# One group of sink scores for two units, sink rows of v by GpSimd transfers, and a new order of work

## The chip, the cores and the metric

The kernel runs on one core of a Trainium2 chip. The metric is device time in microseconds, as a median over several runs. All times of the profile come from one profiled execution and are counted from the start of its span.

## What is computed

Windowed attention with a few always-visible "sink" keys, followed by a channel-mix feed-forward block, for 4 sequences of 768 positions, 8 heads of 64:

```python
scores = scale * q @ k.T                       # per sequence and head
keep   = (key position < 4) | (0 <= query - key < 128)
a      = softmax(where(keep, scores, -1e9))
x      = (a @ v), heads side by side           # [4, 768, 512]
x_prev = x shifted by one position
xk, xr = mu_k*x + (1-mu_k)*x_prev, mu_r*x + (1-mu_r)*x_prev
k      = relu(xk @ w_k)                        # 512 -> 1024
out    = sigmoid(xr @ w_r) * ((k*k) @ w_v)     # 1024 -> 512, and 512 -> 512
```

Inputs and output are float32; the products run in bfloat16.

## The kernel before

A *unit* is 256 positions of one sequence, so there are 12 units, and unit `u` is the part `T = u % 3` of sequence `b = u // 3`. For each unit the kernel does five stages, each made of small operations:

- **load**: k, q and v rows by transfers that SyncE (SP) issues (line 337 for k and q, line 307 for v); the feed-forward weights come by line 354 in five transfers of 1 MB and are cast to bfloat16 by `cast` (line 501 on ScalarE, 505 and 507 on VectorE).
- **prepare**: cast k, q and v to bfloat16 (lines 536 to 543 and 646), turn k and q so that the head dimension lies on the partitions, in early units by TensorE (`transpose`, line 576, four 128x128 pieces) with a copy out of PSUM (`evacuate`, line 589), in later ones by a transposing transfer.
- **attend**: for two head pairs at a time the scores (line 721), the exponential on ScalarE (line 775), the mask on VectorE (line 789; units 0 and 1 add a bias by TensorE instead, line 728), the products with v (line 808), the reciprocal and the division (lines 822 and 825).
- **mix**: turn x by TensorE (line 849), copy it out (line 858), difference and two interpolations on VectorE (lines 877 and 888).
- **ffn** of the unit before: keys (line 939), relu (949 or 953), square (963 or 967), gate (979) with tanh (985), product (997, for the last half unit 909), last multiplication (1006, 919) and the store.

**Sinks.** The window of a unit with T > 0 doesn't reach the first four keys, so they are handled apart. `sink_keys` (line 670, GpSimd) copies the four key columns of every head into `ksink`, zero elsewhere. `sink_scores` (line 696) multiplies them by q of one unit: four matmuls of 256 columns, one for each head pair, each filling 32 of the 128 partitions of a bank. One exponential (line 703) gives `es`. The line 676 matmul `spread` x `vb` puts the four sink rows of v where `es` needs them, and line 680 multiplies by `hmask` into `vsink` on VectorE. `sink_values` (line 763) then adds es x vsink to the outputs. Groups of sink scores exist for T = 1 and for T = 2: eight in all. There is one `ksink`/`vsink` pair for each sequence.

**Order.** Every operation has a number, in the order in which the program text creates it. `CHOICE` says which engine takes an operation that several could do, `ORDER` is the order in which all are issued (each engine keeps its part of that order), `SLOTS` says which buffer of a pool each takes. All three were written by a planner. A negative number in `ORDER` is a filler: a 512-column matmul on zeros (line 1018) that does no work of the reference. `ORDER` holds 30 of them. SP's and GpSimd's queues are in order too: what waits at the head holds up what is behind it.

**GpSimd at the start** makes the constants: `make_ident`, `make_hmask`, `make_bias0`, `make_bias1`, `make_spread`, `make_mask`, `make_mask0`, `make_sinks`. VectorE first does the fills `fill` (with `ones`) and `fill_later` (with `ksink` and `vsink`).

Of the kernel before, what the change touches and what calls it, by code (L numbers as in the profile page):

```python
# [18 lines left out]
    92: "ACT", 93: "ACT", 94: "ACT", 95: "ACT", 97: "ACT", 100: "ACT", 102: "DVE", 105: "DVE",  # L19
    110: "DVE", 111: "DVE", 114: "ACT", 115: "DVE", 139: "POOL", 142: "POOL", 145: "POOL", 148:  # L20
    "DVE", 150: "DVE", 151: "ACT", 152: "ACT", 154: "DVE", 161: "DVE", 191: "DVE", 193: "DVE",
    194: "DVE", 197: "DVE", 199: "DVE", 200: "DVE", 203: "DVE", 204: "DVE", 213: "DVE", 230:
    "ACT", 234: "ACT", 273: "DVE", 276: "DVE", 279: "DVE", 282: "DVE", 285: "ACT", 286: "ACT",
    298: "DVE", 306: "DVE", 315: "ACT", 354: "DVE", 364: "ACT", 365: "DVE", 367: "DVE", 383:
    "ACT", 387: "ACT", 436: "DVE", 439: "DVE", 444: "DVE", 445: "DVE", 467: "ACT", 475: "ACT",
    514: "DVE", 516: "DVE", 521: "DVE", 524: "ACT", 525: "ACT", 546: "ACT", 550: "ACT", 554:
    "ACT", 558: "ACT", 595: "DVE", 598: "DVE", 603: "ACT", 604: "ACT", 606: "DVE", 634: "ACT",
    681: "DVE", 682: "DVE", 691: "DVE", 700: "ACT", 704: "ACT", 708: "ACT", 755: "DVE", 759:
    "DVE", 760: "ACT", 772: "DVE", 781: "ACT", 785: "ACT", 789: "ACT", 834: "DVE", 836: "DVE",
    837: "DVE", 853: "ACT", 856: "DVE", 857: "ACT", 860: "DVE", 861: "ACT", 904: "DVE", 906:  # L30
    "DVE", 910: "DVE", 912: "DVE", 913: "DVE", 929: "ACT", 933: "ACT", 940: "DVE", 941: "ACT",
    994: "DVE", 995: "ACT", 999: "ACT", 1003: "ACT", 1007: "ACT", 1022: "DVE", 1026: "DVE",
    1034: "DVE", 1035: "ACT",
# [13 lines left out]
JOINT = ()  # L47
# [138 lines left out]
def kernel(  # L186
# [19 lines left out]
    NS = 4  # L206
# [199 lines left out]
    def fill_later():  # L406
        for t in ksink + vsink:
            nc.vector.memset(t, 0.0)
# [666 lines left out]
```

## Time and profile before

| what | value |
|---|---|
| median of 3 runs | 165.88 us (165.59 to 166.65) |
| span of the profiled execution | 164.3 us; its time outside the span is not recorded (the median is 1.58 us above the span) |
| busy: PE / DVE / ACT / POOL | 158.4 / 145.4 / 131.2 / 13.5 us |
| instructions: PE / DVE / ACT / POOL | 1603 / 381 / 218 / 38 |
| granted TensorE clock, mean | 0.999 |
| moved | 34.60 MB, mean 211 GB/s |

PE is TensorE, DVE is VectorE, ACT is ScalarE, POOL is GpSimd, SP is SyncE; SPq and POOLq are their queues. A row of a group reads: line, engine, operation, output<-input, shapes, count | busy us, mean ns of one | idle before it. The duration of a matmul includes its way through the array, and neighbours overlap; the pace of a row of matmuls is better read in the chain, where each piece begins where the last one ended.

### The profile page before, as it was taken

The page shows a single profiled execution, that of the slowest core. Times are in us where ns is not written, and L with a number is a line of the kernel's source. Part 1 is how long each engine was busy: PE and PEld are TensorE (multiplying, and loading weights), DVE is VectorE, ACT ScalarE, POOL GpSimd, SP SyncE. Part 2 cuts the span into 40 slices and gives each one's busy share as a digit, 9 for nine tenths or more (in the row PEclk, how much of TensorE's full clock was granted, in tenths as well). Part 3 has the DMA queues.
Part 4 walks back from the last instruction along what each step waited for, and adds up shares of the span by engine and source line. Part 5 has one row for each costly group of instructions (what it writes and reads, how often), then busy time and mean ns, then how long its engine had stood idle before and what let it go on. Part 6 is the DMA issues. An engine that isn't in the chain of part 4 may idle for free.

```text
span 164.3 us, 4195 instructions
## 1 busy us (share of the span) xinstructions
PE 158.4 (96%) x1603; PEld 102.6 (62%) x1603; DVE 145.4 (89%) x381; ACT 131.2 (80%) x218; POOL 13.5 (8%) x38
## 2 busy tenths in 40 slices
PE   6999889999999999999999999999999999999992
PEld 2455568866467587577566775856575765664851
DVE  5259999999999999989999999999999999789752
ACT  3277999999999999999999999997668759163240
POOL 6409300010000000060000000000000000000000
PEclk9999999999999999999999999999999999999999
DMA  4999999999969896999999887986996955077743
GB/s 120 247 305 311 348 335 355 301 354 210 228 154 270 135 240 148 234 198 167 224 216 157 188 156 163 235 146 150 199 123 136 362 149 200 0 90 297 262 185 128
DMA packets 79042, 34.60 MB, mean 211 GB/s; under 512 B 67112, under 2 KB 73520, under 8 KB 79024
## 3 DMA queue, kind: packets, MB, share of 16 engines
q1 hardware_dynamic: 79008, 34.35, 86.3%
q8 instruction: 12, 0.20, 0.6%
q14 instruction: 6, 0.05, 0.1%
q10 hardware_dynamic: 16, 0.00, 0.0%
HBM read 24.12 MB, written 6.29 MB: 185 GB/s over the span
## 4 chain that ended last, share of the span: by engine, by line
PE 79%; ACT 8%; SPq 4%; DMA 3%; issue 2%; DVE 1%; POOL 1%; DVEq 0%; ACTq 0%; POOLq 0%
PE bank L997 23%; PE bank L939 23%; PE bank L979 12%; PE bank L808 6%; PE sc L721 6%; SPq L337 3%; DMA qs<-in_q_dram 3%; PE bank L576 2%; ACT e L775 2%; PE bank L849 2%; ACT rl L949 1%; PE bank L763 1%; ACT qt L589 1%; PE bank L909 1%; PE bank L1018 1%
## 5 line engine op out<-in xcount | busy, mean ns | idle before, releaser
L775 ACT ACTIVATE e<-sc 128x1024 bf16<-128x1024 f32 (+1 forms) x48 | 46.1, 994 | 1.8 <-PE sc L721 1.7
L939 PE MATMUL bank<-xk,wk_sb 128*128 128x256 bf16 x384 | 47.1, 273 | 0.0
L997 PE MATMUL bank<-wv_h,kk 128*128 128x512 bf16 x184 | 43.1, 379 | 0.1
L939 PEld LDWEIGHTS <-wk_sb 128*128 128x128 bf16 x384 | 36.4, 98 | 7.4 <-issue 0.4
L949 ACT ACTIVATE rl<-bank 128x512 bf16<-128x512 f32 x40 | 24.2, 625 | 8.6 <-PE bank L939 7.1
L997 PEld LDWEIGHTS <-kk 128*128 128x128 bf16 x184 | 17.1, 98 | 17.8 <-issue 0.4
L789 DVE TENSOR_TENSOR e<-e,mask 128x1024 bf16<-128x1024 bf16 (+1 forms) x40 | 25.4, 642 | 0.7 <-ACT e L775 0.5
L979 PE MATMUL bank<-wr_sb,xr 128*128 128x512 bf16 x96 | 23.7, 379 | 0.0
L888 DVE SCALAR_TENSOR_TENSOR xk<-td,mu_all,xt 128x256 bf16<-128x256 bf16 x48 | 22.4, 483 | 0.3
L888 DVE SCALAR_TENSOR_TENSOR xr<-td,mu_all,xt 128x256 bf16<-128x256 bf16 x48 | 22.1, 475 | 0.2
L967 ACT ACTIVATE kk<-rl 128x512 bf16<-128x512 bf16 x29 | 18.3, 664 | 4.2 <-DVE rl L953 4.0
L985 ACT ACTIVATE th<-bank 128x512 f32<-128x512 f32 x24 | 15.1, 646 | 5.7 <-PE bank L979 5.7
L825 DVE TENSOR_TENSOR x<-bank,rec 128x256 bf16<-128x256 f32 x48 | 19.2, 416 | 0.4
L808 PE MATMUL bank<-vb,e 128*128 128x65 bf16 x352 | 16.6, 194 | 0.0
L1006 DVE SCALAR_TENSOR_TENSOR w<-th,bank 128x512 f32<-128x512 f32 x19 | 13.0, 682 | 3.6 <-issue 1.8
L808 PEld LDWEIGHTS <-e 128*128 128x128 bf16 x352 | 13.6, 97 | 3.5
L979 PEld LDWEIGHTS <-xr 128*128 128x128 bf16 x96 | 8.8, 98 | 8.6 <-issue 0.2
L721 PE MATMUL sc<-qt,kt 64*128 64x128 bf16 (+1 forms) x256 | 13.9, 238 | 0.0
L721 PEld LDWEIGHTS <-kt 64*128 64x128 bf16 x256 | 8.9, 94 | 5.7 <-issue 3.1
L1018 PE MATMUL bank<-warm 128*128 128x512 bf16 x30 | 10.6, 484 | 1.1 <-DVE warm L1038 1.1
L877 DVE TENSOR_TENSOR td<-xt 128x512 bf16<-128x512 bf16 x24 | 10.3, 428 | 0.7 <-ACT xt L858 0.5
L589 ACT COPY qt<-bank 128x512 bf16<-128x512 bf16 x15 | 9.4, 643 | 1.0 <-PE bank L576 1.0
(74 smaller groups left out, 161.7 us busy)
## 6 DMA issues: line engine op xcount, KB each, us to landing
ks<-in_k_dram SPq DMA_DIRECT2D x24, 256.0 KB, 4.7
qs<-in_q_dram SPq DMA_DIRECT2D x24, 256.0 KB, 4.4
vs<-in_v_dram SPq DMA_DIRECT2D x24, 256.0 KB, 4.4
out_dram<-w SPq DMA_DIRECT2D x19, 256.0 KB, 2.7
w<-in_moe_w_k_dram SPq DMA_DIRECT2D x2, 1024.0 KB, 10.4
w<-in_moe_w_v_dram SPq DMA_DIRECT2D x2, 1024.0 KB, 9.3
w<-in_moe_w_r_dram SPq DMA_DIRECT2D x1, 1024.0 KB, 9.7
out_dram<-ob SPq DMA_DIRECT2D x4, 256.0 KB, 2.6
```

The costliest lines, as they stand in the source:

```text
L721: nc.tensor.matmul(out=sc[:, a, o0:o1], lhsT=lhs[rows], rhs=rhs[rows], start=u not in BIAS, stop=True, skip_group_check=u in BIAS)
L775: nc.scalar.activation(out=buf[ek][:, :, lo:], in_=buf[sck][:, :, lo:], func=AF.Exp, scale=scale)
L789: nc.vector.tensor_tensor(out=at, in0=at, in1=m, op=ALU.mult)
L808: nc.tensor.matmul(out=o[:, g, a, :], lhsT=e[:, a, e0:e0 + 128], rhs=rhs, start=(T == 0 and i == 0), stop=(i == len(blocks) - 1), skip_gro ...
L825: P.op("DVE", dve(256), lambda ok=ok, rk=rk, c=c: nc.vector.tensor_tensor(out=buf["x", u][:, :, 128 * c:128 * c + 128].rearrange("p g (a d ...
L888: nc.vector.scalar_tensor_tensor(out=buf[key][:, c, :], in0=buf[tk][:, i, :], scalar=mu[w][:, c:c + 1], in1=xt[:, c, t0 - 1:t0 + 255], op0 ...
L939: nc.tensor.matmul(out=ps[:, i, :], lhsT=wk_sb[:, c, 128 * f:128 * f + 128], rhs=xk[:, c, :], start=(c == 0), stop=(c == NC - 1), skip_gro ...
L949: nc.scalar.activation(out=buf[rk], in_=buf[psk].rearrange("p (i t) -> p i t", i=2), func=AF.Relu)
L967: nc.scalar.activation(out=buf["kk", u][:, 2 * f2:2 * f2 + 2, :], in_=buf[rk], func=AF.Square)
L979: nc.tensor.matmul(out=buf[psk], lhsT=buf["xr", u][:, c, 128 * g:128 * g + 128], rhs=wr_sb[:, c, :], start=(c == 0), stop=(c == NC - 1))
L985: P.op("ACT", act(512), lambda psk=psk, tk=tk: nc.scalar.activation(out=buf[tk], in_=buf[psk], func=AF.Tanh, scale=0.5), rank + 4 + g, tak ...
L997: nc.tensor.matmul(out=buf[psk], rhs=wv_h[:, f, :], lhsT=buf["kk", u][:, f, 128 * g:128 * g + 128], start=(f == 0), stop=(f == NF - 1))
```

## The change

1. `JOINT = (0, 1, 2, 3)`: sink scores of the units T = 1 and T = 2 of a sequence are one group. Eight matmuls fill both halves of a bank, and one exponential over 512 columns takes the place of two over 256. For this, `prepare` of unit T = 2 is created before `attend` of unit T = 1; the group needs q of both units.
2. `vstage`, a float32 tile, is zeroed by VectorE at the start and gets the four sink rows of v of all four sequences by four transfers that GpSimd issues, one for each of the four positions (32 pieces of 256 bytes each). `vsink` is now `vstage` x `hmask`, by GpSimd or VectorE as `CHOICE` says. `spread`, its making and the matmul of line 676 are gone. In `hmask` and `ksink` too, the four rows of the second head of a pair now lie 16 partitions behind those of the first, not 4.
3. `CHOICE`, `ORDER` and `SLOTS` are new as a whole. The number of operations falls from 1052 to 1043; the 30 fillers stay 30, at other places.

```diff
-JOINT = ()
+JOINT = (0, 1, 2, 3)
...
-    for t in ksink + vsink:
+    for t in ksink + vsink + [vstage]:
         nc.vector.memset(t, 0.0)
...
-            keep(m, -4 * a, [[-32, NP], [0, D + 1]], 1, m)
-            keep(m, 3 + 4 * a, [[32, NP], [0, D + 1]], -1, m)
+            keep(m, -16 * a, [[-32, NP], [0, D + 1]], 1, m)
+            keep(m, 3 + 16 * a, [[32, NP], [0, D + 1]], -1, m)
...
+    for i in range(NS):
+        P.op("POOL", 1000.0, lambda i=i: nc.gpsimd.dma_start(
+            out=vstage[i::16], in_=v[:, :, i, :].rearrange("b h d -> h b d")), -50,
+            service=60.0, descs=32, reads=["stage0"], writes=[("vstage", i)])
...
-        P.op("PE", 220.0, lambda: nc.tensor.matmul(
-            out=buf[psk].rearrange("p (h d) -> p h d", h=H), lhsT=spread,
-            rhs=buf["vb", u][:, 0, :, 0:D], start=True, stop=True), rank + 4, lag=PE_LAG,
...
-        P.op("DVE", dve(512), lambda: nc.vector.tensor_tensor(
-            out=vsink[b % 2][:, :, 0:D], op=ALU.mult, in1=hmask[:, :, 0:D],
-            in0=buf[psk].rearrange("p (h d) -> p h d", h=H)), rank + 4, hold=[psk],
-            reads=[psk, "hmask", "sinks"], writes=[("vsink", b % 2)])
+        def sink_values(engine):
+            return lambda: engine.tensor_tensor(
+                out=vsink[b % 2][:, :, 0:D], op=ALU.mult, in1=hmask[:, :, 0:D],
+                in0=vstage[:, b, :].unsqueeze(1).to_broadcast([128, H, D]))
+
+        P.op("POOL", 1250.0, sink_values(nc.gpsimd), rank + 4, port=True,
+             alts={"POOL": (1250.0, sink_values(nc.gpsimd), True),
+                   "DVE": (dve(512), sink_values(nc.vector), True)},
+             reads=[("vstage", i) for i in range(NS)] + ["hmask", "sinks"],
+             writes=[("vsink", b % 2)])
```

What the new tables say, read by operation number:

- **Engines.** Operations with a choice, before to after: k and q casts ACT 20 to 14, DVE 25 to 27, POOL 3 to 7; v casts ACT 11 to 13, DVE 13 to 6, POOL 0 to 5; relu ACT 40 to 45, DVE 8 to 3; square ACT 29 to 24, DVE 19 to 24; weight casts ACT 6 to 4, DVE 4 to 5, POOL 0 to 1; turned x out of PSUM ACT 10 to 8, DVE 8 to 10. `vsink`: one on DVE (sequence 0), three on POOL.
- **SP's first transfers**: q of unit 0 comes ahead of k, and one transfer of k of unit 1 ahead of v of unit 0; later the second half of w_k ahead of the first, and q of unit 3 ahead of w_r.
- **POOL's order at the start**: bias0, transfer 2, mask0, ident, bias1, transfers 1 and 3, both v casts of unit 0, hmask, sinks, ksink, transfer 0, v cast, mask, v cast, w_k cast, and so on. DVE does `fill_later` ahead of `fill`.
- **PE's order** up to the first keys (line 939): before, the second half of unit 2's k is turned only after the first two key operations and unit 2's scores come after four of them; now all of unit 2's turning and the first of its two score operations come ahead. Of the 30 fillers, 23 stood ahead of the last transpose of unit 0 and 7 behind it; now it is 15 and 15. Two of the last five stand ahead of the first key operation, two behind the second one, and one between the second score operation of unit 2 and the third key operation.

More of the change, by code (lines that the diff above doesn't have):

```diff
@@ L18 @@
 CHOICE = {
[L19 to L30, printed above, removed]
@@ L31 @@
-    "DVE", 910: "DVE", 912: "DVE", 913: "DVE", 929: "ACT", 933: "ACT", 940: "DVE", 941: "ACT",
-    994: "DVE", 995: "ACT", 999: "ACT", 1003: "ACT", 1007: "ACT", 1022: "DVE", 1026: "DVE",
-    1034: "DVE", 1035: "ACT",
+    95: "DVE", 96: "ACT", 97: "ACT", 98: "POOL", 99: "DVE", 100: "ACT", 101: "DVE", 102: "ACT",
+    103: "DVE", 104: "DVE", 105: "DVE", 107: "DVE", 108: "DVE", 110: "ACT", 111: "DVE", 113:
+    "DVE", 114: "DVE", 116: "DVE", 117: "POOL", 118: "POOL", 120: "DVE", 141: "ACT", 143: "ACT",
@@ new lines @@
+    144: "DVE", 146: "ACT", 147: "DVE", 149: "ACT", 150: "DVE", 152: "ACT", 153: "POOL", 154:
+    "POOL", 156: "DVE", 163: "DVE", 169: "DVE", 171: "ACT", 172: "ACT", 174: "DVE", 175: "ACT",
+    177: "ACT", 178: "ACT", 180: "ACT", 181: "DVE", 182: "DVE", 208: "DVE", 215: "DVE", 223:
+    "ACT", 224: "DVE", 227: "ACT", 228: "DVE", 231: "ACT", 232: "ACT", 235: "ACT", 236: "ACT",
+    273: "DVE", 275: "ACT", 276: "DVE", 278: "ACT", 279: "DVE", 281: "ACT", 282: "POOL", 284:
+    "ACT", 285: "ACT", 286: "DVE", 288: "POOL", 290: "DVE", 297: "DVE", 305: "ACT", 306: "ACT",
@@ new lines @@
+    309: "ACT", 310: "DVE", 313: "ACT", 314: "DVE", 317: "ACT", 318: "ACT", 353: "DVE", 355:
+    "ACT", 357: "ACT", 358: "DVE", 360: "ACT", 362: "ACT", 363: "ACT", 364: "ACT", 366: "DVE",
+    373: "ACT", 381: "ACT", 382: "ACT", 385: "ACT", 386: "ACT", 389: "ACT", 390: "DVE", 393:
+    "ACT", 394: "ACT", 407: "DVE", 409: "DVE", 411: "ACT", 412: "ACT", 414: "DVE", 416: "ACT",
+    417: "DVE", 418: "ACT", 446: "ACT", 453: "ACT", 461: "ACT", 462: "DVE", 465: "ACT", 466:
+    "DVE", 469: "ACT", 470: "DVE", 473: "ACT", 474: "DVE", 511: "POOL", 513: "ACT", 515: "ACT",
@@ new lines @@
+    516: "DVE", 518: "DVE", 520: "ACT", 521: "ACT", 522: "ACT", 524: "POOL", 526: "ACT", 533:
+    "ACT", 541: "ACT", 542: "DVE", 545: "ACT", 546: "ACT", 549: "ACT", 550: "ACT", 553: "ACT",
+    554: "ACT", 589: "POOL", 591: "ACT", 593: "ACT", 594: "DVE", 596: "POOL", 598: "ACT", 599:
+    "ACT", 600: "ACT", 602: "ACT", 609: "DVE", 617: "ACT", 618: "ACT", 621: "ACT", 622: "DVE",
+    625: "ACT", 626: "DVE", 629: "ACT", 630: "ACT", 643: "ACT", 645: "DVE", 647: "ACT", 649:
+    "POOL", 651: "DVE", 652: "ACT", 680: "ACT", 687: "DVE", 695: "ACT", 696: "ACT", 699: "ACT",
@@ new lines @@
+    700: "ACT", 703: "ACT", 704: "DVE", 707: "ACT", 708: "DVE", 745: "DVE", 747: "POOL", 749:
+    "POOL", 751: "DVE", 753: "POOL", 754: "DVE", 756: "POOL", 758: "ACT", 765: "DVE", 773: "ACT",
+    774: "ACT", 777: "ACT", 778: "ACT", 781: "ACT", 782: "DVE", 785: "ACT", 786: "ACT", 821:
+    "ACT", 823: "DVE", 825: "ACT", 827: "DVE", 829: "ACT", 830: "ACT", 845: "DVE", 846: "DVE",
+    849: "ACT", 850: "ACT", 853: "ACT", 854: "DVE", 857: "ACT", 858: "DVE", 871: "ACT", 873:
+    "DVE", 875: "DVE", 877: "DVE", 879: "ACT", 880: "ACT", 921: "ACT", 922: "ACT", 925: "ACT",
@@ L34 @@
+    926: "ACT", 929: "ACT", 930: "ACT", 933: "ACT", 934: "DVE", 985: "ACT", 986: "DVE", 989:
+    "ACT", 990: "DVE", 993: "DVE", 994: "ACT", 997: "ACT", 998: "DVE", 1013: "ACT", 1014: "DVE",
+    1017: "ACT", 1018: "DVE", 1021: "ACT", 1022: "ACT", 1025: "DVE", 1026: "ACT",
 }
@@ L390 @@
     ident = tile1([128, 128], BF16, "ident")
-    spread = tile1([128, 128], BF16, "spread")
     hmask = tile1([128, H, D + 1], BF16, "hmask")
@@ L395 @@
     vsink = [tile1([128, H, D + 1], BF16, f"vsink{i}") for i in range(2)]
+    vstage = tile1([128, B, D], FP32, "vstage")
     xts = [tile1([128, NC, S + 16], BF16, f"xt{i}") for i in range(2)]
@@ L400, in fill @@
     def fill():
-        for t, value in ((ones, 1.0), (spread, 0.0), (hmask, 1.0)):
+        for t, value in ((ones, 1.0), (hmask, 1.0)):
             nc.vector.memset(t, value)
@@ L414 @@
     const_op("DVE", 500.0, fill, ["ones0"], rank=-80)
-    const_op("DVE", 1800.0, fill_later, ["sinks0", "ones", "edges"], rank=-79)
+    const_op("DVE", 1800.0, fill_later, ["sinks0", "stage0", "ones", "edges"], rank=-79)
     def keep(out, base, pattern, multiplier, in_=ones, fill=0.0):
@@ L446, in make_bias1 @@
         window_mask(early.bitcast(BF16)[:, 384:640], warm[:, 0:128], LOW)
-    def make_spread():
-        for a in range(2):
-            nc.gpsimd.tensor_copy(
-                out=spread[0:NS, :].rearrange("p (c w) -> p c w", w=32)[:, :, 4 * a:4 * a + NS],
-                in_=ident[0:NS, 0:NS].unsqueeze(1).to_broadcast([NS, NP, NS]))
     def make_hmask():
@@ L479 @@
     const_op("POOL", 1250.0, make_mask0, ["mask0"], ["ones0"], rank=-55)
-    const_op("POOL", 200.0, make_spread, ["spread"], ["ident", "ones0"], rank=-54)
     const_op("POOL", 1400.0, make_hmask, ["hmask"], ["ones0"], rank=-53)
@@ L669, in sink_keys @@
                 rows = slice(64 * a, 64 * a + 64)
-                nc.gpsimd.tensor_copy(out=kz[rows, :, 4 * a:4 * a + NS],
+                nc.gpsimd.tensor_copy(out=kz[rows, :, 16 * a:16 * a + NS],
                                       in_=first(rows))
@@ L674, in prepare @@
              reads=["sinks", ("kt", u, 0), ("kt", u, 1)], writes=[("ksink", b % 2)])
-        psk = ("vsp", b)
-        P.op("PE", 220.0, lambda: nc.tensor.matmul(
-            out=buf[psk].rearrange("p (h d) -> p h d", h=H), lhsT=spread,
-            rhs=buf["vb", u][:, 0, :, 0:D], start=True, stop=True), rank + 4, lag=PE_LAG,
-            take=[("bank", psk)], hold=[("vb", u)], reads=["spread", ("vb", u, 0)], writes=[psk])
-        P.op("DVE", dve(512), lambda: nc.vector.tensor_tensor(
-            out=vsink[b % 2][:, :, 0:D], op=ALU.mult, in1=hmask[:, :, 0:D],
-            in0=buf[psk].rearrange("p (h d) -> p h d", h=H)), rank + 4, hold=[psk],
-            reads=[psk, "hmask", "sinks"], writes=[("vsink", b % 2)])
+        def sink_values(engine):
[7 more added lines that the diff above has]
+             writes=[("vsink", b % 2)])
     def attend(u, rank):
```

157 rows, old and new, of tables (ORDER, SLOTS) are left out of this document.

## The prediction

> **What bounds the kernel now.** I read the busy shares first, then the idle time of TensorE's large groups (count | busy us, mean ns | idle before), both on the page:
>
> ```profile
> span 164.3 us, 4195 instructions
> PE 158.4 (96%) x1603; PEld 102.6 (62%) x1603; DVE 145.4 (89%) x381; ACT 131.2 (80%) x218; POOL 13.5 (8%) x38
> L939 PE MATMUL bank<-xk,wk_sb 128*128 128x256 bf16 x384 | 47.1, 273 | 0.0
> L997 PE MATMUL bank<-wv_h,kk 128*128 128x512 bf16 x184 | 43.1, 379 | 0.1
> ```
>
> TensorE is busy 96% and its large groups don't wait. A busy PE need not run at its pace, so next come stretches, cut where the first key matmul starts (24.1), where the chain leaves TensorE (59.6 to 73.1) and where the last matmul ends. After the length stand PE, PEld, DVE, ACT and POOL busy, clock, DMA share, GB/s:
>
> ```profile
> 0.00:24.10 24.10, 21.58 (x217) 11.78 (x218) 16.85 (x55) 16.41 (x26) 9.86 (x32) 1.00 0.94 277
> 24.10:59.60 35.50, 35.46 (x379) 24.28 (x377) 34.90 (x92) 35.23 (x58) 0.74 (x2) 1.00 0.98 253
> 59.60:73.10 13.50, 13.39 (x161) 9.81 (x159) 12.70 (x32) 13.40 (x25) 2.50 (x2) 1.00 0.90 194
> 73.10:110.00 36.90, 36.90 (x409) 24.51 (x409) 35.52 (x97) 36.54 (x65) 0.39 (x2) 1.00 1.00 186
> 110.00:161.20 51.20, 51.11 (x445) 32.24 (x443) 45.05 (x110) 29.61 (x49) 0.00 (x0) 1.00 0.69 176
> ```
>
> From 24.1 to 161.2 PE is idle 137.1 - (35.46 + 13.39 + 36.90 + 51.11) = 0.24 us. For the pace, the chain in order of time (start, length, what):
>
> ```profile
> 24.13 0.90 PE bank L939 x8
> 51.95 0.22 PE bank L676
> 54.99 0.55 PE sc L721 x12
> 55.54 0.22 PE bank L696 x4
> 58.84 0.22 PE bank L576 x4
> 64.64 0.50 ACT kb L536
> 66.57 0.50 ACT rl L949
> 67.06 0.28 ACT es L703
> 67.34 0.92 ACT e L775
> 68.75 0.48 ACT qt L589
> 121.75 0.22 PE bank L676
> 142.01 3.49 PE bank L939 x32
> ```
>
> Late in the run, where nothing competes, a key matmul takes 3.49 / 32 = 0.109 us; at 24.13 it takes 0.90 / 8 = 0.113. And where the chain runs over ScalarE, the timeline has
>
> ```profile
> 68.80 2.78 PE L939 MATMUL bank<-xk,wk_sb 128*128 128x256 bf16 x24
> ```
>
> which is 0.109 each too, if the last one counts with its whole passage of 0.273. So from 24.1 on the kernel is a row of matmuls at full pace; ScalarE and VectorE, 97 to 99% busy up to 110, just keep up. Time can be won in three ways only: fewer matmuls after 24.1, more useful matmuls before it, or a shorter end, which the new order leaves as it is (the same four quarter products, multiplication, store).
>
> **The change, part by part.**
>
> *The `spread` matmul goes.* Four times 0.22 us (L676 rows of the chain). One of the four lies before 24.1, where PE has fillers and waits, and is worth nothing there; three lie in the full stretch: -0.66 us.
>
> *Sink scores in one group.* PE does eight matmuls of 256 columns per sequence as before: 0.22 for four (L696), with no gap on either side, so 0. ScalarE does one exponential of 512 columns, 0.50 by the relu of the same size, for two of 0.28: 4 x 0.06 = 0.2 us of work off the path, 0.
>
> *`vsink` and the casts that move.* VectorE loses three of the four multiplications
>
> ```profile
> L680 DVE TENSOR_TENSOR vsink<-bank,hmask 128x512 bf16<-128x512 f32 x4 | 2.7, 678 | 0.2 <-PE bank L676 0.2
> ```
>
> 2.0 us, and ScalarE some casts. Neither sets the end, so 0, unless POOL takes it back. From about 25 us on, POOL gets twelve operations that it didn't have: one weight cast, seven q or k casts, a v cast and three multiplications, beside its `ksink` copies. What POOL costs here shows in
>
> ```profile
> engine op xcount: duration ns min/median/max, first and last start us, forms
> L670 POOL COPY ksink<-kt x8: 188/196/2303, 16.2 to 96.6; 64x16 bf16<-64x16 bf16 x8
> 12.64 0.86 POOL L543 CAST qb<-qs 128x512 bf16<-128x512 f32 x1 [6.67 <-DMA qs<-in_q_dram]
> 13.48 0.62 POOL L543 CAST kb<-ks 128x512 bf16<-128x512 f32 x1
> 13.75 0.62 DVE L877 TENSOR_TENSOR td<-xt 128x512 bf16<-128x512 bf16 x1
> L877 DVE TENSOR_TENSOR td<-xt 128x512 bf16<-128x512 bf16 x24 | 10.3, 428 | 0.7 <-ACT xt L858 0.5
> ```
>
> The same tiny copy takes 0.19 or 2.30 us, so POOL can be held up by 2.1; and a VectorE difference beside a POOL cast took 0.62 instead of 0.43, so VectorE can be held up by 0.19. If each of the twelve costs VectorE 0.2 to 0.8 (from the row to a whole cast), that is 2.4 to 9.6 us, against 2.0 saved. VectorE's idle time in the stretches up to 110 is 0.6 + 0.8 + 1.4 = 2.8 us, and 6.2 follow after it. I take 0.2 each, about even: 0 on the path. Bounds: -0.3 (a cleared VectorE hides the last 0.24 us of PE's idle time) to +2.1 (one held-up POOL operation that something needs at once).
>
> The Trainium skill, "SBUF — State Buffer", section "SBUF: two separate sides", says that GpSimd and a VectorE operation that reads two SBUF inputs share a port pair as an exclusive lock, and that the other "fully blocks". The 2.30 us copy agrees. The difference's 0.62 us doesn't settle it: it lost 0.19 us beside a cast of 0.62. By the lock taken whole, the last bound would be the rule and not the exception; that is the third rival below.
>
> *The four GpSimd transfers.* No GpSimd transfer is in this trace. Issuing one holds POOL for something between the shortest POOL instruction above, 0.19, and the hold-up of 2.3; I take 0.6 to 0.7, the nearest rows, which are SP's issues below. Transfers 2, 1 and 3 stand among the constants. `ident` was ready 2.2 us into the span. Now bias0 (0.81 + 0.30), a transfer that waits until `fill_later` has zeroed `vstage` (about 2.6, by the fills' old lengths), and mask0 (like bias0) stand ahead of it: 2.6 + 0.65 + 1.1 + 0.9 = 5.3. PE needs it behind eleven fillers, whose early pace is about 2.74 / 6 = 0.45, so at 1.13 + 5.0 = 6.1: hidden, with 0.8 to spare, and not if a transfer takes 1.5. The v casts of unit 0 wait behind three transfers until about 8.5, but v itself arrives only later. Transfer 0 stands behind `ksink`, about 14.5, and `vsink` of sequence 0 reaches the head of VectorE's queue at about 18.5. Loads here take 4.4 us from issue to landing (vs row), so 14.5 + 0.6 + 4.4 = 19.5 at worst, 1 us of wait with all of VectorE behind it; at best none. I take 0.
>
> ```profile
> 0.81 0.74 SPq L337
> 2.27 0.61 SPq L337
> 2.01 0.18 POOL L424 CAST ident<-ident 8x8 f32<-8x8 bf16 x1
> 3.92 0.81 POOL L418 TENSOR_SCALAR_AFFINE_SELECT ob<-warm 128x128 bf16<-128x128 bf16 x3
> 4.68 0.30 POOL L434 MEMSET ob<- 4x256 bf16 x1
> 1.13 2.74 PE L1018 MATMUL bank<-warm 128*128 128x512 bf16 x6 [1.13 <-DVE warm L1038]
> vs<-in_v_dram SPq DMA_DIRECT2D x24, 256.0 KB, 4.4
> ```
>
> "DMA: Bandwidth & Descriptors" of the Trainium skill, section "Anatomy of one DMA — SWDGE (gpsimd) path", gives about 2.0 us fixed for such a transfer; by that the landing is at 17 and the wait nothing. No run here shows it yet.
>
> *The order up to the first keys.* ScalarE sets them, by the w_k cast:
>
> ```profile
> GB/s 120 247 305 311 348 335 355 301 354 210 228 154 270 135 240 148 234 198 167 224 216 157 188 156 163 235 146 150 199 123 136 362 149 200 0 90 297 262 185 128
> 12.80 1.51 ACT L775 ACTIVATE e<-sc 128x768 bf16<-128x768 f32 x2 [0.55 <-PE sc L721]
> 22.85 1.08 ACT L501 ACTIVATE wk_sb<-w 128x1024 bf16<-128x1024 f32 x1
> ```
>
> Before, from the exponentials of unit 0's second half at 12.80 to the end of the cast at 23.93. Now v of unit 0 has one 256 KB load more ahead of it, 0.85 us at the 305 GB/s of the third slice below, and unit 0's products wait for it. I take 0.35 for the start, between 0 (the load isn't what they wait for) and 0.85. Its list up to the cast: 1.5 for the two small exponentials, 4 x 0.92, seven copies of turned q and k at 0.48, three casts at 0.50, one `es` 0.50, one cast 0.95: 11.5. It ends at 13.15 + 11.5 = 24.7, so the first keys come about 0.8 later. But PE has done more by then: the first scores of unit 2 (0.55) and its last transpose (0.22), which followed the first keys before. Net +0.03.
>
> *Behind the first keys.* PE does two key operations and a transpose (8 x 0.113 + 0.22 = 1.1), and then wants unit 2's second scores, which wait for two exponentials, 2 x 0.92, that follow the cast on ScalarE: 1.84 - 1.1 = 0.7 us of gap, which the order fills with fillers. The other half of w_k comes second and is cast by VectorE behind unit 1's division. Between 0 (ScalarE runs ahead) and 1.5 (this cast late too); I take 0.5.
>
> *Sum.* -0.66 + 0.03 + 0.5 = -0.1: a span of 164.2. The profiled execution's time outside its span isn't given; the median lies 165.88 - 164.3 = 1.58 above it. That makes 165.8; 165.7 with half of the small gains that I put at 0.
>
> **The rivals.**
>
> *The head gains.* PE's fillers before 24.1 are time without work:
>
> ```profile
> L1018 PE MATMUL bank<-warm 128*128 128x512 bf16 x30 | 10.6, 484 | 1.1 <-DVE warm L1038 1.1
> ```
>
> If ScalarE isn't late, the 0.77 us pulled ahead is a gain, no gap follows, and with -0.66 it makes -1.4 to -2.0: 163.9 to 164.5. For it: the four v casts of units 0 and 1 go from ScalarE and VectorE to POOL. Against: ScalarE got more copies and casts before the w_k cast, not fewer.
>
> *Staging comes late, so the change moves a wait and removes none.* Transfer 0 lands at 19.5 or later; VectorE stands at `vsink`, and unit 2's casts and the differences behind it slip by 1 to 2 us, with the keys: about 166.9. For it: POOL held up as in the 2.30 us row; against: 4 us between issue and need.
>
> *POOL's lock, slower.* VectorE's back-to-back work from 30 to 110 holds up POOL by up to 2.1 us an operation, or POOL's casts hold up VectorE by their length, 9.6 us. It decides from the point where VectorE's loss passes the 2.0 saved and the 2.8 idle up to 110, or where a q, k or v cast is needed within 2 us. Price: 9.6 - 2.0 - 2.8 = 4.8, of which I let half be made up after 110, so 2.4; or one hold-up on the path, 2.1. That is about 168, 167.3 to 168.5. For it: the 2303 ns; against: the twelve operations are spread over 100 us.
>
> **How the numbers follow.** Forecast case, 165.0 to 166.5: 0.45. Head gains, 163.9 to 164.5: 0.2. Late staging, 166.5 to 167.3: 0.15. Lock, 167.3 to 168.5: 0.2. One per cent, 1.66 us, is about what a measurement tells from no change. Faster by more than that is below 164.2, over half of the second case and a little beyond: 0.17. Slower by more is above 167.5, nearly all of the last case and the edge of the third: 0.22. Same: 0.61. The range for 8 in 10 leaves out the outer part of both sides: 164.0 to 168.0.
>
> **What would show it.** In the profile after: L676 gone; PE idle time from the first keys to the last matmul still under 1 us plus one gap of about 0.5 just behind the first keys; these at 24.5 to 25.2; POOL busy 25 to 32 us, with single operations above 2 us where VectorE has no pause; `vsink` of sequence 0 at about 18.5 on VectorE with little wait before it; DVE's sum within 3 us of 145.4. I would be wrong if the first keys start before 24 or after 26, or if PE's pace or idle time changes between 30 and 110.

## The result, and the profile after

The changed kernel takes **170.87 us** (median of 4 runs, 170.03 to 172.23) where the kernel before took 165.95 beside it: a ratio of 1.029 [1.026, 1.033]. It is slower by 4.9 us, and outside the range that was given. (Here and below a median is over all runs of a kernel, while a ratio leaves out runs over 1.5% above the fastest of the same kernel, so the two needn't agree to the last digit.)

The page of the changed kernel (its lines are mostly numbered 10 to 12 higher than before, and in the experiments by a few more or fewer: keys 950, scores 732, fillers 1029, `vsink` 686, the transfers 491):

```profile
span 169.2 us, 4186 instructions
PE 158.4 (94%) x1583; PEld 102.5 (61%) x1599; DVE 145.3 (86%) x376; ACT 127.5 (75%) x206; POOL 25.9 (15%) x53
PEclk9999957999999999999999999999999999999999
```

TensorE and VectorE are busy for as long as before, in a span that is 4.9 us longer: in the sum nothing works longer, something waits. The clock has a dent in two slices, 21 to 30 us. The timeline there, over POOL, VectorE and TensorE (start, length, what, in brackets the idle time before it and what ended it):

```profile
14.23 0.56 POOL L491 DMA_DIRECT2D vstage<-in_v_dram  x1
20.00 0.88 DVE L686 TENSOR_TENSOR vsink<-vstage,hmask 128x512 bf16<-128x512 f32 x1 [2.07 <-DMA vstage<-in_v_dram]
21.13 0.41 DVE L553 CAST kb<-ks 128x512 bf16<-128x512 f32 x1
21.61 0.61 PE L586 MATMUL bank<-ident,kb 128*128 128x128 bf16 x4 [2.74 <-DVE kb L553]
22.70 1.04 PE L732 MATMUL sc<-qt,kt 64*128 64x256 bf16 x12
29.06 0.60 PE L950 MATMUL bank<-xk,wk_sb 128*128 128x256 bf16 x4
```

GpSimd issues the transfer of sink row 0 at 14.23. VectorE reaches `vsink` at 17.93 and stands 2.07 us. The cast of unit 2's k is behind it, and TensorE stands 2.74 us for that cast; then it works slowly: twelve score matmuls take 1.04 us where the timeline of before, which also has the first keys, shows 0.62:

```profile
19.57 0.62 PE L721 MATMUL sc<-qt,kt 64*128 64x256 bf16 x12
23.98 1.05 PE L939 MATMUL bank<-xk,wk_sb 128*128 128x256 bf16 x8
```

The windows (length, PE, PEld, DVE, ACT, POOL busy, clock, DMA share, GB/s) give the clock, and the stretch from the first keys to the last matmul, first of after and then of before:

```profile
20.00:25.00 5.00, 3.39 (x31) 1.78 (x32) 4.31 (x8) 2.37 (x5) 1.45 (x2) 0.59 1.11 342
25.00:30.00 5.00, 5.00 (x69) 3.81 (x68) 3.67 (x12) 3.74 (x5) 0.46 (x1) 0.73 1.12 326
29.10:165.97 136.87, 135.26 (x1356) 89.28 (x1370) 125.89 (x319) 111.07 (x182) 12.90 (x17) 1.00 0.85 191
```

```profile
24.10:161.20 137.10, 136.86 (x1388) 90.85 (x1385) 128.17 (x328) 114.78 (x193) 3.62 (x6) 1.00 0.87 200
```

The stretch is as long as before (136.9 and 137.1 us) and begins 5.0 us later. So in this execution the whole loss lies ahead of the first keys, in what is called the head below. The windows of 5 us average the clock: in windows of 1 us it is 0.50 from 21 to 27 us, and 1.00 again from 28. (A few matmul records are missing in some traces: complete, the stretch has 1372 in the new order. With 16 fewer, its busy time reads somewhat too small.)

### The profile page after: what moved, and what is told of

Read it like the earlier page. It is cut to its first block, busy times and chain, and to the rows that moved or that the text cites. A ratio compares the mean times of both kernels' runs of the same rounds, so it can differ in the third digit from the quotient of the medians.

```text
span 169.2 us, 4186 instructions
## 1 busy us (share of the span) xinstructions
PE 158.4 (94%) x1583; PEld 102.5 (61%) x1599; DVE 145.3 (86%) x376; ACT 127.5 (75%) x206; POOL 25.9 (15%) x53
## 4 chain that ended last, share of the span: by engine, by line
PE 71%; DVE 11%; DMA 9%; SPq 2%; issue 2%; POOL 2%; DVEq 0%
PE bank L1008 22%; PE bank L950 19%; PE bank L990 10%; PE bank L819 7%; PE sc L732 6%; DMA vs<-in_v_dram 3%; DMA vstage<-in_v_dram 3%; DVE xk L899 3%; DMA xt<-x 2%; SPq L349 2%; PE bank L860 2%; PE bank L586 2%; PE bank L774 1%; DVE xr L899 1%; DVE e L800 1%
## 5 line engine op out<-in xcount | busy, mean ns | idle before, releaser
L786 ACT ACTIVATE e<-sc 128x1024 bf16<-128x1024 f32 (+1 forms) x48 | 44.0, 957 | 4.1 <-PE sc L732 4.0
L960 ACT ACTIVATE rl<-bank 128x512 bf16<-128x512 f32 x45 | 26.2, 605 | 15.1 <-PE bank L950 13.8
L899 DVE SCALAR_TENSOR_TENSOR xk<-td,mu_all,xt 128x256 bf16<-128x256 bf16 x48 | 23.8, 520 | 0.1
L899 DVE SCALAR_TENSOR_TENSOR xr<-td,mu_all,xt 128x256 bf16<-128x256 bf16 x48 | 22.8, 495 | 0.0
L996 ACT ACTIVATE th<-bank 128x512 f32<-128x512 f32 x24 | 14.2, 602 | 5.1 <-PE bank L990 4.6
L819 PEld LDWEIGHTS <-e 128*128 128x128 bf16 x352 | 14.3, 100 | 4.0 <-issue 0.8
L1017 DVE SCALAR_TENSOR_TENSOR w<-th,bank 128x512 f32<-128x512 f32 x18 | 12.2, 679 | 4.3 <-DMA out_dram<-w 2.0
L978 ACT ACTIVATE kk<-rl 128x512 bf16<-128x512 bf16 x24 | 14.8, 632 | 0.4 <-DVE rl L964 0.3
L833 DVE RECIPROCAL rec<-bank 128x4 f32<-128x4 f32 x48 | 8.0, 175 | 4.8 <-PE bank L819 3.9
L599 ACT COPY qt<-bank 128x512 bf16<-128x512 bf16 x14 | 8.2, 601 | 4.4 <-PE bank L586 4.3
```

Source lines behind the costliest of these rows:

```text
L786: nc.scalar.activation(out=buf[ek][:, :, lo:], in_=buf[sck][:, :, lo:], func=AF.Exp, scale=scale)
L819: nc.tensor.matmul(out=o[:, g, a, :], lhsT=e[:, a, e0:e0 + 128], rhs=rhs, start=(T == 0 and i == 0), stop=(i == len(blocks) - 1), skip_gro ...
L899: nc.vector.scalar_tensor_tensor(out=buf[key][:, c, :], in0=buf[tk][:, i, :], scalar=mu[w][:, c:c + 1], in1=xt[:, c, t0 - 1:t0 + 255], op0 ...
L960: nc.scalar.activation(out=buf[rk], in_=buf[psk].rearrange("p (i t) -> p i t", i=2), func=AF.Relu)
L978: nc.scalar.activation(out=buf["kk", u][:, 2 * f2:2 * f2 + 2, :], in_=buf[rk], func=AF.Square)
L996: P.op("ACT", act(512), lambda psk=psk, tk=tk: nc.scalar.activation(out=buf[tk], in_=buf[psk], func=AF.Tanh, scale=0.5), rank + 4 + g, tak ...
```

## The experiments

Two causes offered themselves, the late transfer and the new order around it; a third was GpSimd's new load. All ratios are to the kernel before on the same chip; its medians there lie between 166.01 and 166.33 us, so a difference of a few tenths between medians of different experiments says nothing.

**1. The transfer early.** Operation 89, the transfer of row 0, goes to the three others, which are issued by 8 us:

```diff
-  ..., 92, -1, ...   174, 87, 119, 89, 153, 88, ...
+  ..., 92, 89, -1, ...   174, 87, 119, 153, 88, ...
```

> Only the place of GpSimd's transfer 0 is changed: it is issued right behind transfers 1 and 3, not behind ksink. Late staging (A): VectorE's wait of 2.07 us at vsink and TensorE's of 2.74 us behind it go, the clock stays at 1.0, the first keys come at 24.5 to 25.5 instead of 29.06, and the time falls by 4 to 5 us to 165.5 to 167. New order (B): the longer lists of ScalarE and VectorE set the first keys; they stay at 28 or later and the time falls by less than 1 us. GpSimd's later work (C): no change before 30 us, 170 to 171.

Measured: 169.25 us, ratio 1.014 [1.006, 1.021]; three runs lie between 167.38 and 169.80, the fourth at 171.41. The profiled execution is the fastest of them:

```profile
span 165.4 us, 4202 instructions
18.18 0.69 DVE L685 TENSOR_TENSOR vsink<-vstage,hmask 128x512 bf16<-128x512 f32 x1
25.27 0.60 PE L949 MATMUL bank<-xk,wk_sb 128*128 128x256 bf16 x4
25.30:162.20 136.90, 136.02 (x1372) 89.41 (x1370) 125.68 (x319) 110.97 (x182) 16.60 (x17) 1.00 0.86 201
```

`vsink` waits for nothing, the clock stays full, and the first keys come 3.8 us earlier. They are still 1.3 later than before. What A said of the wait, the clock and the first keys came true; its time, 165.5 to 167, did not. So late staging is shown, and is not all.

**2. `vsink` later, instead of the transfer earlier** (operation 120 behind the last `xr` of unit 0):

```diff
-  188, 120, 164, 169, 165, 167, 161, 159, 168, 179
+  188, 164, 169, 165, 167, 161, 159, 168, 120, 179
```

> Transfer 0 stays late; VectorE's multiplication into vsink of sequence 0 is moved behind the last interpolation of unit 0, so that nothing needed early stands behind it. A: the cast of unit 2's k comes at about 18.3 instead of 21.1, TensorE doesn't idle there, the clock holds, and the first keys come at 25 to 26: 165.5 to 167.5. B and C: 170 to 171.

169.07 us, 1.016 [1.011, 1.020]: in the median the other way out gives the same. It is not the same path, though. VectorE no longer waits for the transfer, but TensorE now stands 1.06 us for `vsink` itself, with the clock at 1.00, and the first keys come at 26.17, 0.9 later than in experiment 1:

```profile
21.99 0.29 PE L773 MATMUL bank<-vsink,es 64*128 64x130 bf16 x4 [1.06 <-DVE vsink L685]
26.17 0.60 PE L949 MATMUL bank<-xk,wk_sb 128*128 128x256 bf16 x4
```

**3. The wait kept, the clock held up.** Twelve more fillers ahead of unit 2's transpose:

```diff
-  152, 180, 196, 170, 183
+  152, 180, 196, -3, -3, -3, -3, -3, -3, -3, -3, -3, -3, -3, -3, 170, 183
```

> The kernel after with 12 more fillers (12 x 0.216 = 2.6 us) where TensorE idled 2.74 us before unit 2's k is turned; VectorE's wait is untouched. If the idle time made the clock fall, and the clock cost time of its own: granted clock 1.0 in every slice, first keys 1 to 2 us earlier (27 to 28), 169 to 170. If only the wait costs: keys at 29, 170.9. If the fillers are in the way: 171 to 172.

170.49 us, 1.024 [1.020, 1.029], above the 169 to 170 that were expected of the clock. VectorE stood 2.2 us as before, but:

```profile
25.00:30.00 5.00, 5.00 (x69) 3.60 (x67) 4.93 (x14) 4.94 (x7) 0.81 (x1) 1.00 1.13 329
26.94 0.60 PE L950 MATMUL bank<-xk,wk_sb 128*128 128x256 bf16 x4
27.00:165.50 138.50, 136.46 (x1372) 89.36 (x1370) 126.66 (x319) 111.29 (x182) 13.34 (x17) 1.00 0.87 193
89.16 0.62 ACT L546 CAST kb<-ks 128x512 bf16<-128x512 f32 x1 [1.34 <-DMA ks<-in_k_dram]
```

The clock stayed at 1.00 and the keys came 2.1 us earlier than in the changed kernel, yet the end only 0.4. The stretch behind is 1.6 us longer; one place of it is the last row, where ScalarE stands 1.34 us for a load. Here the time won in the head is given back behind it, presumably at places that a late TensorE reached too late to wait at. Experiments 9 to 11 are after them.

**4. GpSimd's load.** Experiment 1, and eleven later casts and multiplications of GpSimd on VectorE:

```diff
-  282: "POOL", 288: "POOL", 511: "POOL", 524: "POOL", 589: "POOL", 596: "POOL", ...
+  282: "DVE", 288: "DVE", 511: "DVE", 524: "DVE", 589: "DVE", 596: "DVE", ...
```

> As e1_early, and the eleven later GpSimd operations with a choice (seven q and k casts, one v cast, three vsink) go to VectorE. C: VectorE and TensorE run freer, 1 to 3 us below e1_early. A alone: VectorE gets some 5 us more work with no lock; 0 to +1 us against e1_early.

169.09 us, 1.017 [1.011, 1.022], as experiment 1, with 16.3 us of GpSimd instead of 29.7. C's 1 to 3 us didn't come: GpSimd's share of the steady work costs nothing that these runs can tell.

**5 and 6. The staging under the old order.** The kernel before with its order, its sink groups and its engines; only the spread matmuls go and four transfers come, once early, once with row 0 late:

```diff
-JOINT = (0, 1, 2, 3)
+JOINT = ()
 ORDER and SLOTS of the kernel before, without `spread` and the four spread matmuls
+  e5: 84, 89, 90, 91, 92, 77      e6: 84, 90, 91, 92, 77, ...  196, 139, 89, 87, 120
```

> The kernel before with its own order, its own sink groups and its own engines; only the source of the sinks' v rows is exchanged: the four spread matmuls go, four GpSimd transfers stand behind the second bias on POOL (issue at about 5.7 us), and VectorE multiplies from the staging tile at the old place (17.4 us). Theory 'late staging and the order': nothing waits, PE loses four matmuls of 0.22 us, so 0.9 less than before, about 165.0 to 165.4. Rival 'the transfers or the read from SBUF cost by themselves' (descriptor work, 0.88 us instead of 0.68 for the multiplication, a shared port): 1.5 to 3 more than before, 167.5 to 169.

> The same, but the transfer of sink row 0 stands ahead of the copy that makes the sinks' ones column, so that it is issued at about 15.5 to 15.8 us and lands, at 5 us of latency, at 20.5 to 21, for a multiplication that stands in VectorE's queue at 17.4. Theory 'late staging': VectorE stands 3 us, PE follows by 2 to 3 us, and with the loss of clock by up to 4: 167.5 to 170 against 165.2 without it. Rival 'the order alone is what is slow': under the old order the wait is taken up by what VectorE has in hand, at most 1 us: under 166.5.

Early: 166.01 us, 0.998 [0.996, 1.001]. Late: 173.22 us, 1.041 [1.038, 1.044]. The pair differs in nothing but the place of one transfer of 8 KB, and by 7.2 us. Late:

```profile
16.05 0.56 POOL L476 DMA_DIRECT2D vstage<-in_v_dram  x1
22.51 0.69 DVE L671 TENSOR_TENSOR vsink<-vstage,hmask 128x512 bf16<-128x512 f32 x1 [4.77 <-DMA vstage<-in_v_dram]
23.59 0.58 PE L845 MATMUL bank<-ident,x 128*128 128x128 bf16 x4 [5.49 <-DVE x L821]
20.00:25.00 5.00, 1.41 (x7) 0.82 (x7) 2.49 (x7) 0.72 (x2) 0.00 (x0) 0.64 1.10 342
25.00:30.00 5.00, 4.57 (x53) 2.83 (x50) 3.00 (x9) 2.57 (x4) 0.00 (x0) 0.68 1.12 340
31.25 1.05 PE L935 MATMUL bank<-xk,wk_sb 128*128 128x256 bf16 x8
```

A wait of 4.8 us on VectorE becomes 5.5 on TensorE and 7.5 at the first keys (31.25; 23.77 in the early one), with the clock at 0.64 and 0.68 meanwhile. So the wait alone, with no new order, is enough for a loss of this kind, and a larger one than the 167.5 to 170 that was expected of it. Early, the staging does neither harm nor good; the gain that was expected, to 165.0 to 165.4, didn't come.

**7. The new order alone**, with the values by the spread matmul again:

```diff
+  P.op("PE", 220.0, ... lhsT=spread, rhs=buf["vb", u][:, 0, :, 0:D] ...)
-  four transfers; vsink of sequences 2 and 3 at their old places
+  vsink of sequences 2 and 3 behind their unit's v casts
```

> The changed kernel with its order, joint sink groups and engines, but with the values by the spread matmul as before: no transfer, no staging tile, all four multiplications on VectorE from PSUM (the first two at their places in the new order, the third and fourth behind their unit's v casts). Theory 'late staging is all of the loss': about that of before, 165.5 to 166.5. Theory 'the new order itself costs the part that early staging did not bring back' (keys 1.3 us later, more waits of TensorE behind them): 167 to 169, like the run with the early transfer.

172.71 us, 1.038 [1.034, 1.041], above both expectations. Inconclusive: TensorE's waits (us in total, times, longest) show that the four matmuls and multiplications, put back by hand, are in the way.

```profile
PE bank L1007 <- DVE vsink L691: 1.5, 1, 1.5
PE bank L587 <- DVE vsink L691: 0.9, 1, 0.9
PE bank L949 <- DVE vsink L691: 0.7, 1, 0.7
```

If these 3.1 us passed to the end in full, which no run shows, it would stand at 169.6 without them, near experiment 1.

**8. VectorE relieved.** Seven late casts to ScalarE under the old order with the early staging, and five under the new order with the early transfer:

```diff
-  e8: 835, 836, 903, 905, 909, 911, 912: "DVE"     e9: 823, 827, 873, 875, 877: "DVE"
+  e8: the same: "ACT"                               e9: the same: "ACT"
```

> The staging alone under the old order, and beside it seven late casts (v of units 10 and 11, k and q of unit 11, 0.42 us each) from VectorE to ScalarE, which is busy 63 to 82% where they stand. Theory 'behind the head TensorE and VectorE bound the kernel together': the 0.9 us that the four spread matmuls gave back were not gained because VectorE, busy at 97 to 99%, comes late by as much; with 2.4 us taken from it the gain appears, 164.9 to 165.4 against 166.0. Rival 'VectorE's late casts are covered': no difference, 165.8 to 166.2.

> The changed kernel with the early transfer, and five late casts (q of unit 10, k and q of unit 11) from VectorE to ScalarE. Theory 'the new order loses behind the head because VectorE is late for TensorE': about 1 us less than the 169.25 of the early transfer alone, near 168. Rival 'what is left of the loss is in the head and in the order's waits before 110 us': no difference, 168.8 to 169.6.

168.16 us, 1.012 [1.009, 1.015], and 169.05, 1.015 [1.009, 1.021]. The first is 2.1 slower than without: TensorE now waits for a v cast that stands in ScalarE's queue (the row below), and both theories about it fell. The second changes nothing. The casts that were taken from VectorE there are not what is left.

```profile
137.49 0.52 PE L804 MATMUL bank<-vb,e 128*128 128x65 bf16 x12 [1.40 <-ACT vb L641]
```

**9. The step at 88 us.** The second kernel of 8 runs level with experiment 1 up to there (its keys even begin 0.1 earlier) and is 2.0 us behind at 91.5. SP's queue, ScalarE and TensorE, first of experiment 1, then of this one:

```profile
82.11 0.57 SPq L328 DMA_DIRECT2D ks<-in_k_dram  x1
85.98 0.63 ACT L545 CAST kb<-ks 128x512 bf16<-128x512 f32 x1
88.06 0.40 PE L706 MATMUL bank<-qt,ksink 128*32 128x256 bf16 x8
```

```profile
83.61 0.58 SPq L328 DMA_DIRECT2D ks<-in_k_dram  x1
88.62 0.62 ACT L545 CAST kb<-ks 128x512 bf16<-128x512 f32 x1 [2.35 <-DMA ks<-in_k_dram]
89.22 0.29 PE L706 MATMUL bank<-qt,ksink 128*32 128x256 bf16 x4 [0.84 <-DMA qt<-qb]
```

The load of unit 8's k, second half, is issued 1.5 us later, lands 5.0 us after that, and ScalarE stands 2.35 us with the exponential of the joint group of units 7 and 8 behind it; the group itself stands 0.84 us for unit 8's turned queries. Twelve profiles have the new order and this load at its place. In five of them ScalarE stands for it, 1.22 to 2.35 us (e3, e4, e10, e13 and this one; the number behind an e is that of the run); in seven, the changed kernel and experiment 1 among them, it doesn't. So this wait comes and goes. Two suspects, then: the joint group and the load. The group later, the groups apart, and one group apart, all on top of experiment 1:

```diff
 e11
-  538, 537, 667, 653, 616, 600, 654, 60, ...  587, 531, ...  57, 651, 588, 674, 644
+  538, 537, 667, 616, 600, 60, ...  587, 588, 531, ...  57, 651, 674, 653, 654, 644
 e13, e14
-JOINT = (0, 1, 2, 3)
+JOINT = ()            e14: (0, 1, 3)
```

> The changed kernel with the early transfer, and with the joint sink group of units 7 and 8 and its exponential moved behind six key groups and the last values of unit 6 (about 2 us later on TensorE; the group needs both units' queries, and unit 8's come by a DMA transpose). In two profiles of its relatives TensorE stood at this group 0.6 to 0.8 us for the transposed queries, and 0.6 us more behind it, and was 2.0 us later at its end than in the one fast profile; up to the group they were even. Theory 'the joint group waits for the queries of the unit after it': nothing waits there in any run, 167.4 to 168.2, and the runs lie closer together than 167.4 to 169.8. Rival 'the order is late elsewhere': the median stays at 168.8 to 169.5.

> The changed kernel's order with the early transfer, but no joint sink groups: each of units 2, 5, 8 and 11 has its own group of four matmuls and its own exponential again, right behind its unit's first scores; the groups of units 1, 4, 7 and 10 stay where the joint ones stood and wait for no other unit's queries. Theory 'what is left of the loss is the joint groups': at most 167.3, the 1.3 us by which the first keys are late. Rival 'it is the order around them (which runs of TensorE's, VectorE's and the DMA queue's work stand next to each other), with the groups joint or apart': 168.5 to 169.8, like the run with the early transfer.

> The same with only units 7 and 8 apart, the place at which two profiles showed a wait of TensorE for unit 8's transposed queries. If that one place is the loss: as with none joint, 167.2 to 168.0, and the step of 1.5 to 2 us between 85 and 92 us is gone from the profile. If not: 168.5 to 169.8.

170.51 us, 1.023 [1.018, 1.027]; 169.80, 1.025 [1.021, 1.029]; 169.07, 1.020 [1.016, 1.024]. None is clearly better than experiment 1, not even with all groups apart, which lies where the rival put it; the group later is above both of its expectations. The joint groups are not the rest of the loss. With units 7 and 8 apart the profile has no step at 88 us, as that of experiment 1 has none, so it doesn't show that parting them removed it. Ten microseconds later TensorE stands for ScalarE, much more briefly:

```profile
98.96 1.02 PE L990 MATMUL bank<-wr_sb,xr 128*128 128x512 bf16 x3 [0.32 <-ACT rl L960]
```

**10. The load earlier.** Operation 54 ahead of unit 9's q load, with the early transfer (e15) and with the late one (e17):

```diff
-  52, 579, 61, 505, ...  535, 581, 582, 54, 657
+  52, 579, 54, 61, 505, ...  535, 581, 582, 657
```

> The changed kernel with the early transfer, and the load of the second half of unit 8's k moved in the SP queue from behind the queries' first transpose to ahead of unit 9's q load (about 3 us earlier). In the profiles of the runs that lost 1.5 to 2 us between 85 and 92 us ScalarE stood 2.2 to 2.4 us for this load at its cast, with the exponential of the joint group behind it; in the one that lost nothing the load had been issued 1.5 us earlier and landed just in time. Theory 'a load with no slack in the new order': that step is gone in every run, 167.2 to 168.0, and the runs lie closer together. Rival 'the next place without slack takes it over': 168.5 to 169.8.

> The changed kernel with its late transfer, and only that load moved. Its profile showed no wait there (TensorE came 4 us later to that place), so the load should change nothing: 170.3 to 171.3. The distance to the run with the early transfer is then the whole price of late staging: theory 3 to 3.8 us, as in the profiled executions; rival 1.6, as in the medians so far.

168.55 us, 1.014 [1.012, 1.017], and 171.11, 1.026 [1.021, 1.031]. With the late transfer the load changes nothing. With the early transfer the six runs lie within 1.0 us of each other (167.89 to 168.86), where three of experiment 1 lay within 2.4 and the fourth higher, and the profile has the cast without a wait:

```profile
80.26 0.57 SPq L328 DMA_DIRECT2D ks<-in_k_dram  x1
86.23 0.63 ACT L545 CAST kb<-ks 128x512 bf16<-128x512 f32 x1
```

The slowest runs are gone, as a missing wait would do it, and none of the three profiles with the load moved (e15, e16, e17) has the wait; four runs against six don't prove it. The median is only 0.7 lower, at the edge of the rival's range, and the intervals don't separate it from experiment 1. The pair e15 and e17 gives the price of late staging in the new order: 171.11 - 168.55 = 2.6 us by the medians (2.0 by the two ratios), with intervals that don't touch. That lies between the two expectations, 3 to 3.8 and 1.6. One of e17's six runs took only 168.84, with a mean clock of 1.00 where the other five have 0.98 to 0.99: the late transfer doesn't cost in every execution. What spared that one was not profiled.

**11. Without the five fillers among the first keys** (-2, -1, -4, -3, -4 between operations 206 and 221), on experiment 1 (e10), on e11 (e12) and on e15 (e16):

> The changed kernel with the early transfer, and without the five filler matmuls among the first keys (two ahead, two and one behind them, 1.1 us of TensorE at full clock). Theory 'the fillers cover waits for VectorE and for the casts of w_k': TensorE stands idle for as long, the same time as with them, 168.9 to 169.6. Rival 'the fillers themselves are the gap': the first forty keys come 0.6 to 1.1 us earlier and the end with them, 168.1 to 168.6.

> The same, and without the five fillers among the first keys, which were 1.0 us in the medians, 0.1 us in the first keys' forty. Theory 'two separate losses': 166.4 to 167.4, then still above before. Rival 'the fillers' microsecond was the scatter of the group's wait': as with the fillers, within 0.3 us of the run beside it.

> The same without the five fillers among the first keys. If the fillers only cover waits: as the run beside it, within 0.3 us. If they cost: 0.5 to 1.0 us less.

168.27 us, 1.013 [1.008, 1.018]; 170.20, 1.015 [1.012, 1.018]; 167.86, 1.011 [1.008, 1.014]. The medians are 1.0, 0.3 and 0.7 us lower than with the fillers; the intervals of the first and the third pair overlap, and the runs of the second kernel scatter from 168.39 to 172.10. In e16's profile the block of forty keys begins 0.45 us earlier than in e15's and stands for the cast of w_k on VectorE:

```profile
27.62 4.54 PE L949 MATMUL bank<-xk,wk_sb 128*128 128x256 bf16 x40 [0.45 <-DVE wk_sb L516]
```

So the fillers partly cover this cast. What they cost by themselves, between nothing and 1 us, these runs don't settle. Nothing that was built beats the kernel before; the staging alone, early, equals it.

## Why the prediction was wrong

**What bounds the kernel**: TensorE's row from the first keys on was the right frame. In the changed kernel too the stretch has its length, and everything hangs on when the keys begin. The bound of "before 24 or after 26" was the right alarm: they begin at 29.06.

**The step that failed** is transfer 0: "19.5 at worst, 1 us of wait with all of VectorE behind it; at best none. I take 0". It landed at 19.88, 5.65 us after its issue began, and `vsink` came to the head of the queue at 17.93, not 18.5. The wait of 2.07 was thus double the stated bound: about half of the excess is the landing, half VectorE's earlier arrival. The value taken was the best end of the range, though the nearest row (4.4 us for a load) gave the worst end. The four transfers of after, in the list of DMA issues (count, KB each, median from issue to landing):

```profile
vstage<-in_v_dram POOLq DMA_DIRECT2D x4, 8.0 KB, 4.6
```

The Trainium skill, "DMA: Bandwidth & Descriptors", section "Anatomy of one DMA — SWDGE (gpsimd) path", gives about 2.0 us fixed for a transfer of this kind, which spoke for that choice; the trace has 4.6 here, and the measurement decides.

**The rival "Staging comes late"** named the mechanism, with too small a price. It priced the wait itself, "1 to 2 us". The runs show 2.0 to 2.6 us in the new order and 7.2 for a wait of 4.8 in the old one. Up to the first keys the traces show why the wait grows: unit 2's cast is behind it, TensorE stands 2.74 us and goes on at half its clock. Of the 3.8 us at the first keys, holding the clock up took back 2.1 (experiment 3). At the end of the run that was worth only 0.4, so how much of the price at the end is the clock's stays open.

**The order up to the first keys**: predicted 0.8 us later, measured 1.3 with the early transfer (25.27 against 23.98). ScalarE's part was right: its cast of w_k was to end at 24.7 and ends at 24.78 in experiment 1. The other half microsecond is two fillers, which the order puts ahead of the first keys and the prediction didn't count. Without them the keys begin at 24.76 (e16), 0.05 after the cast's end at 24.71; in e10, where the cast ends at 25.17, they begin at 25.23.

```profile
23.64 1.14 ACT L510 ACTIVATE wk_sb<-w 128x1024 bf16<-128x1024 f32 x1
24.82 0.60 PE L1028 MATMUL bank<-warm 128*128 128x512 bf16 x2
```

```profile
24.76 0.61 PE L949 MATMUL bank<-xk,wk_sb 128*128 128x256 bf16 x4
```

(The first two rows are of experiment 1, the last one of e16.)

**Spread matmul, -0.66, the 0.77 pulled ahead, and the gap of 0.5**: the two savings were right, the gap too small. In experiment 1 the stretch is 137.1 - 0.66 - 0.77 + 0.65 (three fillers behind the first key operation) + 0.64 (idle time 0.88 instead of 0.24) = 136.96; measured 136.90. So fillers and small waits take 1.3 us where the prediction had 0.5, and the stretch shrinks by 0.2 instead of 0.9. Under the old order the profile shows the spread matmuls' saving too (stretch 136.4 instead of 137.1), while the median gains only 0.1.

**POOL's lock** fell by experiment 4. POOL was busy 25.9 us, within the 25 to 32 that were given, and `qb` casts there took up to 4.1 us (experiment 1), but TensorE has no wait for one of them in that profile. The lock of the Trainium skill, "SBUF — State Buffer", section "SBUF: two separate sides", may make those long casts; no run here separates it. **`ident`** was 0.8 us late for TensorE in the changed kernel's profile, not 0.8 early, because the eleven fillers ahead took 3.85 us and not 5.0 and `ident` came at 5.7, not 5.3; in that of experiment 1 they took 4.88 and TensorE didn't wait. What it cost was not tried.

**The sum as it stands**: of 4.9 us, 2.6 are late staging (e17 against e15; 2.0 by the ratios). The remaining 2.3 belong to the new order with its early transfer. So the forecast would have been too low without late staging too: it had -0.1 there. In the profile of experiment 1, its fastest run, that part is 1.1 us (1.3 at the first keys, -0.2 behind them), and the two fillers and the larger gap account for it. About 1 us is left over in the medians. In five profiles a load without slack at 87 to 89 us held ScalarE for 1.2 to 2.4 us. That such waits follow from the order is shown only place by place, and what sets the last microsecond stays open.

## What to carry to other kernels

A transfer that takes the place of a matmul has to be issued by its landing time, taken from the nearest row of the trace at the same load, and not by its size or by a fixed cost. Where an in-order engine feeds the bounding one, a wait on it can cost more than its length (here 7.2 us for 4.8, and 2.0 to 2.6 for 2.1); so price the wait, the idle time that it makes downstream, and the clock after that, and try it, because the sum need not arrive at the end. When time won ahead doesn't arrive at the end, look for the load with the least slack behind it.

## What was not expected of the hardware

- TensorE's 2.74 us of idle time (18.87 to 21.61) took the granted clock to 0.50 until about 27.7 us; twelve fillers in the wait (idle time 0.28) kept it at 1.00, and it stayed there in experiment 2 with an idle time of 1.06.
- GpSimd transfers of 8 KB in 256-byte pieces took 4.6 us from issue to landing (median; the late one 5.65 from the start of its issue), about as long as loads of 256 KB (4.5 to 5.2), and issuing one held GpSimd 0.60 us in the mean.
- The same `vsink` multiplication took 0.88 us on VectorE in the changed kernel and in experiment 3, and 0.69 in experiments 1, 6 and e17, so early or late isn't what sets it; on GpSimd it took 1.12 to 1.32.
